# A Fourier and expert-layer kernel: dummy rows and half of a table sent later, float64 decoding in five VectorE operations instead of seven

## The chip, the cores and the metric

The kernel runs on one core of a Trainium2 chip. The metric is the time of one execution on the device in microseconds (us), as the median of several runs.

## What is computed

Three stages follow one another. `x` is 8 batches of 3072 tokens of 256 numbers.

```python
X = np.fft.fft(np.fft.fft(x, axis=1), axis=2).real      # attention stage
do_compute = x @ w_skip > 0                             # mixture of experts, 8 experts of 256 -> 1024 -> 256
e_idx = np.argmax(xc @ w_gate, axis=1)                  # for the rows xc that compute
y[mask] = gate_w[mask, None] * (np.maximum(xc[mask] @ w1[e], 0.0) @ w2[e])
out[do_compute] = xc + y
h = x @ w_in                                            # last layer, 256 -> 2048 -> 256
g = (a0 + a1*h + a2*h**2 + a3*h**3) / (1 + |b0|*|h| + |b1|*h**2 + 1e-6)
return g @ w_out
```

`w_in` and `w_out` come as float64; the kernel reads them as pairs of 32-bit words.

## The kernel before

There are two phases. The first computes the Fourier transform of all 24576 tokens, decides the expert of each and scatters the rows into a table in HBM (`xs`), sorted by expert. The second reads the rows back and runs experts and last layer; it fills the time from about 408 us on. The change is in the first phase, but for one loop count at the start of the second.

Products are made in float16 pairs: each float32 value is split into a high part (ScalarE, `AF.Copy`) and a low part (VectorE or GpSimd, a subtraction), and three matmuls are added up.

**The first phase.** `load_x(c)` loads block `c` (a 96x1024 tile; 8 blocks make a batch) from SP's queue into one of four buffers, so block `c+4` can be issued when the split of block `c` is done. `split_hi` (L190; L188 first where GpSimd makes the low part) and `split_lo` (L200 on VectorE, L198 on GpSimd for three blocks of each batch from block 12 on) split it. `s1(c)` is the first part of the transform, 24 matmuls; `s1_hi` (L231) and `s1_lo` (L238 on VectorE for blocks 0 to 6, afterwards two matmuls L241 and L242 on ScalarE) take the result out. A lead-in loop does this for the eight blocks of batch 0. It also issues the four pieces of the twiddle table `twt`.

Then come 98 steps `n` (12 per batch and two more). Step `n` stands for batch `n // 12` and its step `n % 12`, called step 0 to 11 of the batch here. It runs `s2` of two groups of tokens (12 matmuls L256, taken out by L260 on ScalarE and L261 on VectorE), `s3` of the step two before (12 matmuls, L305 to L307; L311 on ScalarE; L312 to L314 on VectorE), and in two of three steps a block of the next batch: `load_x`, `s1`, `split_hi`, and `split_lo` a step later. `s3` needs piece `k` of the twiddle table from the batch's step `3k + 2` on. Four PSUM buffers (`u`) are shared by all these.

**Work on the side** is written as Python generators; a step takes one or more pieces (calls) of each. Engines take their instructions in the order in which they are written, so the place of a piece among the others counts.

- `route_steps(bb)`: from step 1 of the next batch on, one piece per step: maximum, one-hot (L330 to L332), ranks by 25 matmuls (L336, L338), row numbers (L354), then two indirect scatters from GpSimd's queue per step (L357), 24 in all. Scatters need the dummy rows (`dum`), written from SP's queue to `xs` first. Row buffers are reused ten row tiles later, so `s3` writes (L312) wait for scatters.
- `decode_steps()`: `w_in` and `w_out` in eight items of 1024 columns: load from SP's queue (L374, L376), VectorE operations L391 to L398 that make a float32 of two words, ScalarE's high part L402, VectorE's low part L404, and the write to `wd` from ScalarE's queue (L406). Six calls make an item. Then eight items of the first two experts' weights, two calls each (load L415 or L417, high part L426, low part L428, write L430). 64 calls are spread evenly over steps 5 to 87. Loads and the `ws` tile that is written have two buffers each.
- `coefficients()`: tiny operations (L570) from step 12 on.

## Time and profile before

| | us |
|---|---|
| median of three runs | 3132.73 |
| lowest and highest run | 3129.66, 3134.80 |
| the profiled execution, its own time | 3128.56 |
| its span, first to last instruction | 3126.5 |
| TensorE busy in the span | 2981.5 (95%) |
| VectorE busy | 2701.1 (86%) |
| ScalarE busy | 2523.4 (81%) |
| GpSimd busy | 1392.4 (45%) |

The busy time of an engine is that of its instructions, overlaps counted once. All times in the rows are from the start of the span. PE is TensorE, DVE VectorE, ACT ScalarE, POOL GpSimd and SP the engine whose queue issues most transfers; ACTq and SPq are the queues' own issues. A share of the whole span is a mean over phases with different limits, so the rows below are from stretches of the first phase.

### The profile page before, as it was taken

To read this page: it belongs to the slowest core of one execution; us is meant where nothing else is said; L and a number is where in the kernel's file an instruction comes from. 1 tells how busy PE (TensorE), PEld (TensorE's weight loads), DVE (VectorE), ACT (ScalarE), POOL (GpSimd) and SP (SyncE) were. 2 spreads that over 40 slices of the span, in tenths; PEclk is the share of its full clock that TensorE was granted. 3 is DMA by queue.
4 is the path that set the end of the run, shared out by engine and by line. 5 is a ranking of instruction groups with operands and counts; after the bars stand their busy time and mean duration, and the time that the engine had idled before them with its cause. 6 is when DMAs were issued, how large, how long until landed. Compare 5 with 4: busy or idle time off the path is not lost.

```text
span 3126.5 us, 57696 instructions
## 1 busy us (share of the span) xinstructions
PE 2981.5 (95%) x23586; PEld 2198.1 (70%) x23586; DVE 2701.1 (86%) x2929; ACT 2523.4 (81%) x2694; POOL 1392.4 (45%) x796
## 2 busy tenths in 40 slices
PE   6899879998999999999999999999999999999996
PEld 5777647776767777777777777777777777777764
DVE  5999788999888898989888788898889888888886
ACT  5777667887888888878888788888888888888884
POOL 0467665443343444434444444444434444344444
PEclk9999989999999999999999999999999999999998
DMA  8556743121111221112112100020011000200000
GB/s 210 170 175 181 239 136 102 31 82 58 35 55 31 75 65 34 55 58 72 41 36 73 38 28 22 13 80 11 28 48 43 23 11 28 75 18 15 11 11 14
DMA packets 75617, 198.09 MB, mean 63 GB/s; under 512 B 12243, under 2 KB 36180, under 8 KB 72404
## 3 DMA queue, kind: packets, MB, share of 16 engines
q1 hardware_dynamic: 54612, 135.42, 14.5%
q0 software_dynamic: 18432, 50.55, 4.6%
q10 hardware_dynamic: 2304, 8.39, 0.7%
q8 instruction: 186, 3.05, 0.4%
q14 instruction: 83, 0.68, 0.1%
HBM read 190.69 MB, written 77.05 MB: 86 GB/s over the span
## 4 chain that ended last, share of the span: by engine, by line
PE 73%; DVE 12%; ACT 6%; issue 4%; DMA 3%; POOL 1%; SPq 0%; ACTq 0%; POOLq 0%; DVEq 0%
PE u L886 34%; PE accz L896 26%; PE acc L896 9%; DVE gh L995 3%; DVE T L977 2%; PE u L256 2%; DMA out<-ob,ids 1%; PE ut L876 1%; DVE V L1000 1%; ACT Y L976 1%; ACT T L975 1%; DMA xt<-in_x 1%; POOL xs L357 1%; DVE gl L1007 1%; ACT V L981 1%
## 5 line engine op out<-in xcount | busy, mean ns | idle before, releaser
L1001 POOL TENSOR_TENSOR V<-T,V 128x1024 f32<-128x1024 f32 x384 | 911.9, 2375 | 1395.6 <-DVE V L1000 1345.9
L896 PE MATMUL accz<-wo,gh 128*128 128x256 f16 x6144 | 1031.5, 273 | 2.8 <-ACT ob L1023 2.8
L886 PE MATMUL u<-th,wi 128*128 128x512 f16 x3072 | 984.1, 382 | 37.3 <-DVE T L977 31.2
L896 PE MATMUL accz<-wo,gl 128*128 128x256 f16 x3072 | 839.3, 273 | 14.5 <-DVE gl L1007 13.7
L886 PEld LDWEIGHTS <-wi 128*128 128x128 f16 x4608 | 453.2, 98 | 509.9 <-issue 54.5
L977 DVE SCALAR_TENSOR_TENSOR T<-T,co,u 128x1024 f32<-128x1024 f32 x384 | 490.2, 1277 | 303.5 <-ACT Y L976 299.0
L896 PEld LDWEIGHTS <-gh 128*128 128x128 f16 x6144 | 602.7, 98 | 155.5 <-issue 5.1
L975 ACT ACTIVATE T<-u,co 128x1024 f32<-128x1024 f32 x384 | 462.9, 1206 | 280.4 <-PE u L886 266.0
L995 DVE SCALAR_TENSOR_TENSOR gh<-T,co,Y 128x1024 f16<-128x1024 f32 x384 | 650.0, 1693 | 0.0
L886 PE MATMUL u<-tl,wi 128*128 128x512 f16 x1536 | 586.6, 382 | 0.1
L1007 DVE SCALAR_TENSOR_TENSOR gl<-V,co,Y 128x1024 f16<-128x1024 f32 x384 | 489.4, 1275 | 20.3 <-POOL V L1001 20.3
L1000 DVE SCALAR_TENSOR_TENSOR V<-V,co,gh 128x1024 f32<-128x1024 f32 x384 | 490.1, 1276 | 0.0
L985 ACT ACTIVATE Y<-V,co 128x1024 f32<-128x1024 f32 x384 | 443.1, 1154 | 0.0
L981 ACT ACTIVATE V<-Y,co 128x1024 f32<-128x1024 f32 x384 | 440.9, 1148 | 0.3 <-DVE gl L1007 0.3
L976 ACT ACTIVATE Y<-u,co 128x1024 f32<-128x1024 f32 x384 | 428.1, 1115 | 0.0
L989 ACT ACTIVATE Y<-Y 128x1024 f32<-128x1024 f32 x384 | 404.8, 1054 | 0.0
L896 PEld LDWEIGHTS <-gl 128*128 128x128 f16 x3072 | 301.3, 98 | 53.2 <-DVE gl L1007 16.4
L886 PE MATMUL u<-th,mw 128*128 128x256 f16 x1664 | 293.1, 275 | 10.6 <-DMA mw<-wd 5.6
L1024 POOL DMA_INDIRECT out<-ob,ids x192 | 225.7, 1175 | 125.4 <-ACT ob L1023 73.5
L896 PE MATMUL acc<-mw,hh 128*128 128x256 f16 x1664 | 278.1, 273 | 0.0
L886 PEld LDWEIGHTS <-mw 128*128 128x128 f16 x2496 | 246.0, 99 | 41.3 <-DMA mw<-wd 6.1
L930 ACT ACTIVATE hh<-u 128x1024 f16<-128x1024 f32 x104 | 106.5, 1024 | 158.3 <-PE u L886 158.3
(207 smaller groups left out, 3542.4 us busy)
## 6 DMA issues: line engine op xcount, KB each, us to landing
mw<-wd SPq DMA_DIRECT2D x50, 2048.0 KB
xt<-in_x SPq DMA_DIRECT2D x64, 384.0 KB
xm<-xs SPq DMA_DIRECT2D x52, 258.0 KB
wf<-in_moe_w SPq DMA_DIRECT2D x48, 256.0 KB
wd<-ws SPq DMA_DIRECT2D x48, 256.0 KB
xt<-xs SPq DMA_DIRECT2D x22, 516.0 KB
wd<-ws ACTq DMA_DIRECT2D x16, 512.0 KB
wr<-in_moe_w_in SPq DMA_DIRECT2D x4, 1024.0 KB
```

The costliest lines, as they stand in the source:

```text
L886: pe.matmul(u[:, s, :], lhsT=sta, rhs=mv[:, k, :], start=(n == 0), stop=(n == 5))
L896: pe.matmul(acc[:, r, :], lhsT=sta[:, c], rhs=mv, start=(first and r % 2 == 0 and s == 0 and n == 0), stop=(last and s == nf - 1 and n == ...
L975: act.activation(d["T"], d["u"], AF.Square, scale=A[0], bias=A[1])
L976: act.activation(d["Y"], d["u"], AF.Abs, scale=A[4])
L977: dve.scalar_tensor_tensor(out=d["T"], in0=d["T"], scalar=A[2], in1=d["u"], op0=ALU.add, op1=ALU.mult)
L981: act.activation(d["V"], d["Y"], AF.Square, bias=A[5])
L985: act.activation(d["Y"], d["V"], AF.Ln, bias=A[6])
L989: act.activation(d["Y"], d["Y"], AF.Exp, scale=-1.0)
L995: dve.scalar_tensor_tensor(out=h[:], in0=d["T"], scalar=A[a0], in1=d["Y"], op0=ALU.add, op1=ALU.mult)
L1000: dve.scalar_tensor_tensor(out=d["V"], in0=d["V"], scalar=A[c], in1=h[:], op0=ALU.add, op1=ALU.mult)
L1001: pool.tensor_tensor(out=d["V"], in0=d["T"], in1=d["V"], op=ALU.subtract)
L1007: dve.scalar_tensor_tensor(out=l[:], in0=d["V"], scalar=A[a0], in1=d["Y"], op0=ALU.add, op1=ALU.mult)
```

## The change

1. The five writes of dummy rows, issued ahead of the steps before, are issued in steps 5, 7, 9, 11 and 13. Of the four pieces of the twiddle table two are issued in the lead-in (after blocks 5 and 7) and two in steps 2 and 4. The cosine table `csb` is issued ahead of blocks 2 and 3, and the copies from it stand ahead of three other small VectorE operations. The first weight load of the decoding is issued ahead of the steps.
2. In the lead-in, the low parts of blocks 3 and 5 go by the way of L241 and L242 instead of L238.
3. Decoding: a ScalarE pass (`AF.Abs`) takes the place of the masking L397; the sign bit and the exponent's top bit are kept by other masks, and the exclusive-or L395 is gone. Five calls make an item, with the low part and the write in one. An item of the experts' weights takes one call: low part, write, a load two items on, and the high part of the next item.
4. The calls are made one per step in steps 2 to 11 of batch 0, and from then on twice in step 0, once in steps 1 and 6 and twice in step 9 of each batch.
5. The routing has an empty piece between the one-hot and the matmuls that read it, so what follows comes a step later. The second phase takes one more piece of the last batch's routing at its start.

```diff
@@ s1_lo
-                if c < 7:
+                if c < 7 and c not in (3, 5):
@@ route_steps, behind the one-hot
             yield
+            yield
             u = new_u()
@@ decode_steps
             nxt = load(0)
+            yield
             for n in range(8):
...
-                m = wp.tile([128, 1024], I32, tag="wm", name="wm")
+                m = wp.tile([128, 1024], F32, tag="wm", name="wm")
-                dve.tensor_scalar(out=fi, in0=hw, scalar1=3, scalar2=0x7FFFFFFF, op0=ALU.logical_shift_left, op1=ALU.bitwise_and)
-                dve.scalar_tensor_tensor(out=fi, in0=hw, scalar=-0x80000000, in1=fi, op0=ALU.bitwise_and, op1=ALU.bitwise_or)
+                act.activation(m[:], hw.bitcast(F32), AF.Abs)
+                dve.tensor_scalar(out=fi, in0=hw, scalar1=3, scalar2=0x3FFFFFFF, op0=ALU.logical_shift_left, op1=ALU.bitwise_and)
+                yield
+                dve.scalar_tensor_tensor(out=fi, in0=hw, scalar=-0x40000000, in1=fi, op0=ALU.bitwise_and, op1=ALU.bitwise_or)
                 yield
                 dve.scalar_tensor_tensor(out=fi, in0=lw, scalar=29, in1=fi, op0=ALU.logical_shift_right, op1=ALU.bitwise_or)
-                dve.tensor_scalar(out=fi, in0=fi, scalar1=0x40000000, scalar2=None, op0=ALU.bitwise_xor)
-                yield
-                dve.tensor_scalar(out=m[:], in0=hw, scalar1=0x7FFFFFFF, scalar2=None, op0=ALU.bitwise_and)
-                dve.scalar_tensor_tensor(out=f[:], in0=m[:], scalar=float(0x38100000), in1=f[:], op0=ALU.is_ge, op1=ALU.mult)
+                if n + 1 < 8:
+                    nxt = load(n + 1)
                 yield
+                dve.scalar_tensor_tensor(out=f[:], in0=m[:], scalar=TINY, in1=f[:], op0=ALU.is_ge, op1=ALU.mult)
                 act.activation(st[:, 0, :], f[:], AF.Copy, scale=sc)
                 yield
                 dve.scalar_tensor_tensor(out=st[:, 1, :], in0=f[:], scalar=sc, in1=st[:, 0, :], op0=ALU.mult, op1=ALU.subtract)
-                yield
                 act.dma_start(out=WD[E + n // 4, :, n % 4, :, :], in_=st[:])
                 yield
...
+            pend = hi()
+            yield
+            for n in range(4 * EARLY):
+                t, st = pend
                 dve.scalar_tensor_tensor(out=st[:, 1, :], in0=t, scalar=256.0, in1=st[:, 0, :], op0=ALU.mult, op1=ALU.subtract)
-                yield
                 act.dma_start(out=WD[n // 4, :, n % 4, :, :], in_=st[:])
+                if n + 2 < 4 * EARLY:
+                    loads.append(load_e(n + 2))
+                if loads:
+                    pend = hi()
+                yield
@@ lead-in
-            if c >= 4:
-                g = 6 * (c - 4)
-                sp.dma_start(out=twt[:, g:g + 6], in_=tw[:, g:g + 6])
+            if c in (5, 7):
+                load_tw(c // 7)
@@ steps
-            while decoded < min(n_dec, (n - 3) * n_dec // 84):
-                next(prep, None)
-                decoded += 1
+            for _ in range(1 if n < 12 else DECODE.get(gp, 0)):
+                if n >= 2:
+                    next(prep, None)
+            if n in (2, 4):
+                load_tw(2 + n // 4)
+            if n in (5, 7, 9, 11, 13):
+                dummies((n - 5) // 2)
```

`DECODE` is `{0: 2, 1: 1, 6: 1, 9: 2}`, and `TINY` is the float32 with the bits 0x38100000.

Three places show how this moves instructions. The first is SP's queue from block 4 of x to the first weight loads (`xt` is a block of x, `twt` the table, `dum` the dummy rows, `wr` a weight load). Before:

```order
L178 DMA xt<-in_x 96x1024
L585 DMA twt<-const_tw 128x3072
L589 DMA xs<-dum 512x1x258 x4
L591 DMA xs<-dum 768x1x258
L178 DMA xt<-in_x 96x1024 x4
L374 DMA wr<-in_moe_w_in 128x2048 x2
L178 DMA xt<-in_x 96x1024 x6
```

And with the change:

```order
L180 DMA xt<-in_x 96x1024 x6
L584 DMA twt<-const_tw 128x3072
L180 DMA xt<-in_x 96x1024 x2
L584 DMA twt<-const_tw 128x3072
L377 DMA wr<-in_moe_w_in 128x2048
L180 DMA xt<-in_x 96x1024 x2
L584 DMA twt<-const_tw 128x3072
L180 DMA xt<-in_x 96x1024 x2
L377 DMA wr<-in_moe_w_in 128x2048
L584 DMA twt<-const_tw 128x3072
L589 DMA xs<-dum 512x1x258
```

The `x4` block of x behind the five dummy writes is that of blocks 12 to 15. With the change, block 12 is the first behind the first weight load, and the first dummy write stands behind block 15.

The second place is VectorE in step 3 of batch 3, the one-hot of the routing (L330 to L332 before, L332 to L334 after). Before:

```order
L314 TENSOR_TENSOR rt<-ev,u 128x18
L330 TENSOR_TENSOR rt<-rt 128x24x8
L331 TENSOR_SCALAR rt<-rt 128x24
L332 TENSOR_TENSOR rt<-rt,smt 128x216
L397 TENSOR_SCALAR wm<-wr 128x1024
L398 SCALAR_TENSOR_TENSOR wf<-wm,wf 128x1024
L570 TENSOR_TENSOR co<-co,rt 128x1
L261 SCALAR_TENSOR_TENSOR o2l<-u,o2h 128x552
```

With the change, this step and the next:

```order
L332 TENSOR_TENSOR rt<-rt 128x24x8
L333 TENSOR_SCALAR rt<-rt 128x24
L334 TENSOR_TENSOR rt<-rt,smt 128x216
L580 TENSOR_TENSOR co<-co,rt 128x1
L263 SCALAR_TENSOR_TENSOR o2l<-u,o2h 128x552
L314 TENSOR_TENSOR mw_71<-ev,u 128x2x129
L315 TENSOR_TENSOR mw_71<-ev,u 128x2x127
L316 TENSOR_TENSOR rt<-ev,u 128x18
L580 TENSOR_SCALAR co<-co 128x1
L580 RECIPROCAL rt<-co 128x1
L263 SCALAR_TENSOR_TENSOR o2l<-u,o2h 128x552
```

The two decoding operations behind the one-hot are gone from the step, and the step after it holds no routing.

The third is ScalarE at the end of a step with an expert's weights in batch 6. Before:

```order
L190 ACTIVATE xh<-xt 96x1024
L430 DMA wd<-ws 128x2048
L426 ACTIVATE ws<-wr 128x1024
L231 ACTIVATE o1h<-u 128x192x4
L260 ACTIVATE o2h<-u 128x552
```

With the change, step 9 of that batch, which has two calls:

```order
L313 ACTIVATE ev<-u 128x276
L434 DMA wd<-ws 128x2048
L426 ACTIVATE ws<-wr 128x1024
L434 DMA wd<-ws 128x2048
L426 ACTIVATE ws<-wr 128x1024
L233 ACTIVATE o1h<-u 128x192x4
```

The second write and the second high part now stand between the first ones and the next step's evictions, and each write waits for the low part that VectorE makes in the same call.

## Rows read from the trace of the kernel before

**Rows 1.** Busy us (instructions) per stretch; then granted clock, DMA share, GB/s.

```profile
0.00:30.00 30.00, 16.84 (x218) 15.91 (x219) 19.04 (x33) 17.30 (x19) 1.06 (x8) 1.00 0.87 226
30.00:63.20 33.20, 21.57 (x225) 16.75 (x224) 9.64 (x18) 16.20 (x23) 2.12 (x1) 0.79 1.05 255
63.20:83.70 20.50, 20.08 (x249) 16.57 (x248) 20.07 (x36) 16.88 (x26) 0.00 (x0) 1.00 0.30 79
83.70:109.20 25.50, 22.23 (x274) 18.03 (x273) 21.46 (x64) 19.23 (x30) 7.10 (x3) 1.00 0.43 136
109.20:128.80 19.60, 19.56 (x249) 16.53 (x249) 18.71 (x42) 16.51 (x25) 11.64 (x10) 1.00 0.64 204
128.80:156.40 27.60, 22.18 (x274) 18.05 (x273) 24.92 (x67) 20.51 (x31) 20.01 (x16) 1.00 0.64 192
...
176.00:204.30 28.30, 23.49 (x274) 19.07 (x273) 23.30 (x63) 20.22 (x32) 21.70 (x18) 0.94 0.58 190
...
224.30:249.10 24.80, 22.10 (x274) 18.02 (x273) 23.66 (x64) 20.13 (x33) 19.07 (x15) 1.00 0.69 197
...
269.10:297.80 28.70, 22.23 (x275) 18.10 (x274) 27.20 (x65) 20.59 (x31) 21.62 (x17) 1.00 0.51 153
...
317.70:345.70 28.00, 23.65 (x274) 18.95 (x273) 19.98 (x59) 20.84 (x32) 22.68 (x19) 0.94 0.74 225
345.70:366.50 20.80, 19.86 (x249) 16.58 (x249) 17.15 (x37) 15.86 (x24) 11.46 (x12) 1.00 0.49 166
...
390.40:408.00 17.60, 15.23 (x175) 13.23 (x172) 13.17 (x40) 8.09 (x17) 9.75 (x10) 1.00 0.45 159
...
500.00:3126.50 2626.50, 2566.36 (x18989) 1866.64 (x18986) 2293.91 (x1994) 2179.25 (x2210) 1118.69 (x568) 0.99 0.13 42
```

The five busy times are those of TensorE's matmuls, its weight loads, VectorE, ScalarE and GpSimd.

**Rows 2.** Timeline of ScalarE, 0 to 110 us: start, us; [idle before <- releaser].

```profile
54.21 1.06 ACT L188 ACTIVATE xt<-xt 96x1024 f32<-96x1024 f32 x1 [11.02 <-DMA xt<-in_x]
```

**Rows 3.** Timeline of SP's queue, 18 to 60 us: start, us.

```profile
26.07 9.49 SPq L589 DMA_DIRECT2D xs<-dum  x4
35.61 2.19 SPq L591 DMA_DIRECT2D xs<-dum  x1
37.90 5.14 SPq L178 DMA_DIRECT2D xt<-in_x  x4
```

**Rows 4.** Groups of VectorE, 30 to 410 us: busy us, mean ns | idle before.

```profile
L397 DVE TENSOR_SCALAR wm<-wr 128x1024 int32<-128x1024 int32 x8 | 9.8, 1231 | 0.0
L392 DVE SCALAR_TENSOR_TENSOR wf<-wr,wf 128x1024 int32<-128x1024 int32 x8 | 9.8, 1226 | 0.3
L398 DVE SCALAR_TENSOR_TENSOR wf<-wm,wf 128x1024 f32<-128x1024 int32 x8 | 9.8, 1226 | 0.3
...
L391 DVE TENSOR_SCALAR wf<-wr 128x1024 int32<-128x1024 int32 x8 | 5.7, 718 | 0.0
L395 DVE TENSOR_SCALAR wf<-wf 128x1024 int32<-128x1024 int32 x8 | 5.6, 703 | 0.3
```

**Rows 5.** Groups of ScalarE's decoding, 30 to 410 us.

```profile
L426 ACT ACTIVATE ws<-wr 128x1024 f16<-128x1024 f32 x8 | 8.4, 1050 | 7.9 <-DMA wd<-ws 6.1 <-DVE ws L428 1.8
L402 ACT ACTIVATE ws<-wf 128x1024 f16<-128x1024 f32 x8 | 8.4, 1049 | 3.8 <-DVE wf L398 3.8
```

**Rows 6.** Group of TensorE's routing matmuls, 30 to 410 us.

```profile
L336 PE MATMUL u<-rt,utt 128*128 128x216 f16 (+7 forms) x168 | 11.9, 230 | 11.6 <-DVE rt L332 7.6 <-DVE o2l L261 4.0
```

**Rows 7.** Timelines of VectorE and of GpSimd, 194 to 198 us.

```profile
194.77 3.10 DVE L397 TENSOR_SCALAR wm<-wr 128x1024 int32<-128x1024 int32 x1
...
195.16 2.15 POOL L198 TENSOR_TENSOR xl<-xt,xh 96x1024 f16<-96x1024 f32 x1
```

**Rows 8.** Timeline of ScalarE, 368 to 384 us.

```profile
369.81 0.34 ACTq L430 DMA_DIRECT2D wd<-ws  x1
...
381.52 1.06 ACT L426 ACTIVATE ws<-wr 128x1024 f16<-128x1024 f32 x1 [6.07 <-DMA wd<-ws]
```

**Rows 9.** Timeline of VectorE in step 3 of batch 6, 312 to 396 us.

```profile
335.63 2.75 DVE L331 TENSOR_SCALAR rt<-rt 128x24 f16<-128x24 f32 x1
```

More of the change, by code (lines that the diff above doesn't have):

```diff
@@ L38 @@
 CB = 276
+TINY = float(np.int32(0x38100000).view(np.float32))
+DECODE = {0: 2, 1: 1, 6: 1, 9: 2}
 def split16(v):
@@ L380, in decode_steps @@
             nxt = load(0)
-            pend = None
+            yield
             for n in range(8):
                 t = nxt
-                if n + 1 < 8:
-                    nxt = load(n + 1)
                 v = t[:].rearrange("p (n two) -> p n two", two=2)
@@ L450, in program @@
             split_x(c)
-        dve.tensor_copy(out=carry[:], in_=smt[:, 0:9])
-        dve.tensor_copy(out=wgh[:, :, 0, :], in_=wgf[:])
-        dve.tensor_tensor(out=wgh[:, :, 1, :], in0=wgf[:], in1=wgh[:, :, 0, :], op=ALU.subtract)
         for h in range(2):
@@ L457, in program @@
                 dve.tensor_copy(out=f2t[:, h, mv, 147:276], in_=csb[:, h, mv, 1, 0:129])
+        dve.tensor_copy(out=carry[:], in_=smt[:, 0:9])
+        dve.tensor_copy(out=wgh[:, :, 0, :], in_=wgf[:])
+        dve.tensor_tensor(out=wgh[:, :, 1, :], in0=wgf[:], in1=wgh[:, :, 0, :], op=ALU.subtract)
         def gate_columns():
@@ L571, in coefficients, with load_tw, dummies @@
                 yield
+        def load_tw(k):
+            sp.dma_start(out=twt[:, 6 * k:6 * k + 6], in_=tw[:, 6 * k:6 * k + 6])
+        def dummies(r):
+            if r < R0:
+                sp.dma_start(out=XS[SKIP0 + r * TILE:SKIP0 + (r + 1) * TILE, :].rearrange("(p r) c -> p r c", p=128),
+                             in_=dum[:, None, :].to_broadcast([128, 4, ROW]))
+            else:
+                sp.dma_start(out=XS[0:R1 * HALF, :].rearrange("(p r) c -> p r c", p=128), in_=dum[:, None, :].to_broadcast([128, R1 * HALF // 128, ROW]))
         for c in range(8):
@@ L582, in program @@
                 gate_columns()
-            if c >= 4:
-                g = 6 * (c - 4)
-                sp.dma_start(out=twt[:, g:g + 6], in_=tw[:, g:g + 6])
+            if c in (5, 7):
+                load_tw(c // 7)
         s1_hi()
         s1_lo()
-        for r in range(R0):
-            sp.dma_start(out=XS[SKIP0 + r * TILE:SKIP0 + (r + 1) * TILE, :].rearrange("(p r) c -> p r c", p=128),
-                         in_=dum[:, None, :].to_broadcast([128, 4, ROW]))
-        sp.dma_start(out=XS[0:R1 * HALF, :].rearrange("(p r) c -> p r c", p=128), in_=dum[:, None, :].to_broadcast([128, R1 * HALF // 128, ROW]))
         late = []
@@ L594, in program @@
         coeff = coefficients()
-        n_dec = 8 * 6 + 4 * EARLY * 2
-        decoded = 0
+        next(prep)
         c1 = 8
@@ L1158, in program @@
                 if i == 0:
-                    next(last)
-                    next(last)
+                    for _ in range(3):
+                        next(last)
             if 0 <= i - 1 < total:
```

18 lines of the change are left out of this document (9 added, 9 removed).

## The prediction

> **What bounds the kernel now.** I read the table of stretches first, cut at the start of the Fourier steps, six steps to a row [rows 1]. From 500 us to the end TensorE works in 2566.4 of 2626.5 us, and the change touches nothing there. Whatever it does happens in the first 408 us or so, and since the last stage is TensorE's own pace, time saved ahead of it should come out at the end.
>
> In those 408 us three things stand out. The six steps from 30.0 to 63.2 us take 33.2 us, and TensorE works in 21.6 of them; the next six take 20.5. From there on the second halves of the batches, which carry no routing besides its last two pieces, take 19.6 us in batch 1 and 20.8 in batch 6, with TensorE busy nearly throughout: this is the floor of six steps. The first halves, which carry the routing, take 25.5, 27.6, 28.3, 24.8, 28.7 and 28.0 us, on the mean 27.2, with TensorE busy in 22.2 to 23.7 of each.
>
> The timeline of ScalarE says why the early stretch is long: it waits 11.0 us for a block of x and goes on at 54.2 [rows 2]. The timeline of SP says where the block was: SP issues the five writes of dummy rows from 26.07 on, needs 9.49 us for the first four and 2.19 for the fifth, and reaches the next blocks of x at 37.90 only [rows 3]. In the same stretch DMA is busy throughout (share 1.05, 255 GB/s) [rows 1].
>
> The long first halves are VectorE's and the coupling's. VectorE is busy in 21.5 to 27.2 us of those of batches 1 to 5, and decoding is part of it: seven operations per item, with the means of [rows 4] (L394 as L392, L404 as L398) 7.6 us together. TensorE's routing matmuls take 11.9 us in seven batches, 1.7 per batch, and waited 11.6 us in all [rows 6]. That wait falls in first halves alone.
>
> **The change part by part.**
>
> *Dummies and tables.* Up to the block that was late, the trace moved 30 us at 226 GB/s and 24 us at 255, some 12.9 MB [rows 1]. By the shapes of the tiles the change takes 2.9 MB of dummies and half of 3.1 MB of table from ahead of that block and puts one 1.05 MB load of weights there: 3.4 MB less, which at 255 GB/s is 13 us. The block, which landed at 54.2, then lands near 41 us by that count, and earlier if SP issues it earlier, since SP stood 11.7 us in the dummies [rows 3]. ScalarE asked for it at 43.2 us (54.2 less 11.0). So the wait should go whole. The six steps then cost what the next six do, 20.5 us with decoding in them, a gain of 12.7; the low clock granted in that stretch (0.79 on the mean, so a part of it at 1.2 GHz) goes with the idle time. Bounds: 11.0, the wait alone, and 13.6, down to the floor of 19.6. I take 12.5. What is late next: the dummies now go out singly in steps 5 to 13 between blocks of x that are loaded two to three steps ahead, and must land before the first scatter in step 20, seven steps after the last of them, some 23 us at 19.6 us for six. I cost this at nothing; without that cover POOL's scatters would start late by the time of one write, 0.8 MB at 255 GB/s or 3 us. The third and fourth table pieces are issued in steps 2 and 4 and needed in steps 8 and 11.
>
> *The prelude.* One table piece (3 us at 255 GB/s) no longer stands ahead of a late block, the copies of the cosine table run before VectorE waits for small constants, and two subtractions go from VectorE to TensorE and ScalarE. TensorE is busy in 16.8 of 30.0 us there [rows 1]. I take 1 us; bounds -1 and 2.
>
> *Decoding.* Gone are two VectorE operations per item, L395 and L397, 0.70 and 1.23 us; the others stay [rows 4]. ScalarE gets one more pass of the size of L402, 1.05 us [rows 5]. Over eight items VectorE loses 15.5 us of work and ScalarE gains 8.4. VectorE is on the path only where routing lies beside decoding, so the place counts more than the sum. Before, 64 calls are spread over 84 steps, 4.6 to a half batch: at 7.6/6 us, 5.8 us of VectorE in a first half. After, three calls (two in step 0, one in step 1) of 5.6/5 us: 3.4 us. VectorE's mean in batches 1 to 5 of 24.1 us becomes 21.7, below TensorE's 22.2. Nothing of decoding remains in steps 2 to 5, where the one-hot and the ranks are made, and the added yield gives VectorE a whole step between the one-hot and the matmuls that read it. The halves ran 2.9 us over VectorE's busy time. Between 22.2, where all lies beside TensorE, and 26, where ScalarE's new passes in steps 0 and 1 eat the most of it, I take 24.0, nearer the first since the second halves show six steps running at TensorE's pace with VectorE 95% busy. Gain 3.0 us each (27.0 less 24.0), five batches: 15; bounds 5 and 24.
>
> One row shows what else the moved operations met: L397 in step 3 of batch 3 took 3.10 us while GpSimd's subtraction beside it took 2.15 [rows 7]; L395, of the same kind and size, has a mean of 0.70 [rows 4]. So 2.4 us of it was a standstill. In step 3 of batch 6, where no decoding stands, a small routing operation, L331, took 2.75 us [rows 9]. I keep the 15, since most batches have no such row, and the case in which the standstill passes to the next operation is a rival below. The Trainium skill (SBUF — State Buffer, Who interferes with whom) has VectorE and GpSimd share one port pair that one of them holds for a whole instruction while the other stands still. Both rows agree with it.
>
> *Weights of the experts.* These now take one call each instead of two: VectorE's low part, the write on ScalarE's queue, the next load, and ScalarE's next high part. Where two calls stand in one step (batch 6, steps 0 and 9; batch 7, step 0), ScalarE waits in its own order for VectorE (1.2 us) and then for a buffer whose write was issued just before. Behind it stand the evictions that TensorE needs. The trace has such a wait once: write at 369.81, its buffer free at 381.52, ScalarE idle for 6.07 of that [rows 8]. This was beside the 4 MB of weights that the next stage loads; so I take 3 us of standstill at the first two places, half of it hidden by ScalarE's spare time (it is busy in 20.8 of 28.0 us [rows 1]), against the 3 us that batch 6 wins as the others do: 0, with another -1 for chains of VectorE, ScalarE and VectorE in batches 4 and 5. Bounds -7 and 2.
>
> *The tail.* The wait of 6.07 us in batch 7 becomes one of the same kind two steps earlier: nothing. The added yield puts the last scatters one step later, and the last Fourier steps wait for those rows, so the stage ends one short step later: 17.6 us for eight steps [rows 1], 2.2 each. I take -2; bounds -6 and 3.
>
> **Sum:** 12.5 + 1 + 15 - 1 - 2 = 25.5 us. The profiled execution took 3128.56 us (span 3126.5), so 3103.1. The median of the three runs, 3132.73, stands 4.2 above it, so **3107**.
>
> **The rivals.** A difference within 0.2% (6.3 us) can't be told from no change here.
>
> - *Only the stall goes.* The first halves stay at 27 us, because ScalarE in steps 0 and 1 (two passes per block for GpSimd, now a decode pass or a wait for VectorE more) sets them and not VectorE. For it: the first half of batch 6 had VectorE busy in 20.0 us only and still took 28.0 [rows 1]. Against it: ScalarE had 7 us free there. The sum is 12.5 + 1 - 1 - 2 = 10.5: 3122.
> - *The block of x is late again.* The weight load ahead of it and the table pieces hold it as the dummies did. For it: DMA is the limit up to 63 us (share 1.05), and the count above leaves only 2 us. Against it: SP is free 11 us earlier. With half the wait left the sum is 25.5 - 5.5 = 20: 3113; with all of it, 13: 3120.
> - *The standstill at the port is passed on.* GpSimd still subtracts beside steps 1 to 4 of each batch, and what stood still in [rows 7] and [rows 9] is followed by other VectorE operations. At 2.4 us in each of five batches the sum is 25.5 - 12 = 13.5: 3119. The rule named above would have it so; the rows show it in some batches only.
> - *Slower.* The double calls of the expert weights. If each of the three places holds ScalarE as long as that one write took, 11.7 us, and TensorE with it, this costs 35 less the 6 lost before: 29, against the 25.5 of the sum, so 3136. It decides from some 10.5 us of TensorE's time at each place. Against it: L426's eight have 6.1 us of waits for a buffer in total, all from that one place [rows 5].
>
> **How the numbers follow.** Forecast (sum 18 to 36) 0.60; only the stall 0.18; port passed on 0.07; block late again 0.07; slower 0.04, half of it by over 6.3 us; part gains of several lost, down to within 6.3 us, 0.04. The range reaches from 3096, where the halves get near 22.5 us, to 3122, which takes in all rivals but the slower one; what is below or above holds some 0.2. The forecast's own range is 3097 to 3115. Faster 0.92, same 0.06, slower 0.02.
>
> **What would show it.** Right: no wait of ScalarE for x near 43 us and the first six steps near 20.5 us; first halves of batches 1 to 5 near 24 us with TensorE busy in over 90%; second halves at 20; the first stage ending near 383 us instead of 408; the rest unchanged at 2718 us. Wrong: waits of ScalarE for L428's or L404's counterpart ahead of a write in steps 0, 1 and 9, or for a buffer in batches 6 and 7; rows of x waited for after 35 us; or a last stage that starts early and then waits, for the fills of the row table or for expert weights, and gives the time back.

## The result and the profile after

| | us |
|---|---|
| changed kernel, median (lowest to highest of 4 runs) | 3167.24 (3162.78 to 3168.07) |
| kernel before, beside it (4 runs) | 3133.08 (3129.66 to 3134.80) |
| ratio, 95% interval | 1.0107 (1.0090 to 1.0125) |
| profiled execution, its span | 3168.07, 3165.9 |

The change is 34 us slower; 3107 was forecast. The profile after, by stretches that begin at the same Fourier steps as those of [rows 1] (busy us of TensorE's matmuls, its weight loads, VectorE, ScalarE and GpSimd; then granted clock, DMA share, GB/s):

```profile
31.70:53.00 21.30, 20.70 (x225) 16.52 (x224) 11.85 (x21) 16.91 (x24) 2.48 (x1) 0.87 0.77 246
53.00:81.40 28.40, 22.72 (x249) 18.20 (x248) 19.54 (x35) 18.41 (x28) 0.00 (x0) 0.88 0.71 203
81.40:107.10 25.70, 23.16 (x275) 18.68 (x274) 19.00 (x50) 20.63 (x31) 7.21 (x3) 0.93 0.55 155
107.10:134.20 27.10, 23.06 (x250) 18.63 (x248) 18.57 (x55) 16.86 (x25) 10.53 (x10) 0.87 0.40 123
...
187.00:217.10 30.10, 24.46 (x274) 19.75 (x273) 20.12 (x48) 21.13 (x33) 20.95 (x17) 0.89 0.57 178
217.10:236.90 19.80, 19.72 (x253) 16.59 (x250) 17.65 (x53) 15.93 (x24) 12.46 (x12) 1.00 0.61 191
...
369.50:403.90 34.40, 24.08 (x253) 19.29 (x250) 17.81 (x49) 16.24 (x24) 22.43 (x22) 0.80 0.53 177
...
540.00:3165.90 2625.90, 2566.62 (x19004) 1867.50 (x19001) 2295.92 (x1997) 2178.36 (x2210) 1116.47 (x569) 0.99 0.13 42
```

The last row says that the second phase is what it was (2626.5 us before for the same stretch, 2566.4 of TensorE). The first six steps take 21.3 us in place of 33.2: the stall is gone. But the next six take 28.4 where they took 20.5, and the same goes on. The Fourier steps begin 1.7 us later than before; then, against before: first six steps -11.9, next six +7.9, first halves of batches 1 to 5 together +8.2 (25.7, 31.4, 30.1, 28.9, 27.0), their second halves +16.2 (27.1, 21.4, 19.8, 22.2, 24.8, where 19.6 to 20.0 was the rule), batch 6 +15.3, the first half of batch 7 +1.8. That is 39.2 of the span's 39.4 us. More work is not the reason: in most of these stretches VectorE, the suspected one, is busy less than before, and over the span it is busy 15.0 us less (2686.1). ScalarE has 7.9 us more (2531.3), its added pass. TensorE is busy 18.7 us more with the same matmuls; why these take longer stands in the last section.

So it is waits. The groups of the changed kernel, 30 to 420 us, that answer to [rows 5] and [rows 6], with three more (busy us, mean ns | idle before, and what ended it). The window ends in the midst of the last batch's routing, so L339 and L263 lack their last 24 and 10 instructions; up to 460 us L339's idle time is 0.0 still, and L263's is 103.0, of which 102.8 for `o2h`.

```profile
L243 PE MATMUL u<-o1h,nid 128*128 128x384 f16 x114 | 50.8, 551 | 54.0 <-ACT o1h L233 53.5
L339 PE MATMUL u<-rt,utt 128*128 128x216 f16 (+7 forms) x144 | 9.5, 219 | 0.0
...
L190 ACT ACTIVATE xt<-xt 96x1024 f32<-96x1024 f32 x19 | 19.9, 1046 | 0.0
L404 ACT ACTIVATE ws<-wf 128x1024 f16<-128x1024 f32 x8 | 8.4, 1056 | 14.7 <-DVE wf L401 14.7
L426 ACT ACTIVATE ws<-wr 128x1024 f16<-128x1024 f32 x8 | 8.4, 1052 | 20.6 <-DVE ws L433 8.3 <-DMA wr<-in_moe_w 4.7 <-DMA wd<-ws 4.7
...
L263 DVE SCALAR_TENSOR_TENSOR o2l<-u,o2h 128x552 f16<-128x552 f32 x86 | 62.7, 729 | 100.1 <-ACT o2h L262 99.8
```

The first and the last of these in the kernel before, 30 to 410 us:

```profile
L241 PE MATMUL u<-o1h,nid 128*128 128x384 f16 x113 | 46.8, 515 | 21.7 <-ACT o1h L231 21.2
L261 DVE SCALAR_TENSOR_TENSOR o2l<-u,o2h 128x552 f16<-128x552 f32 x96 | 69.8, 727 | 61.2 <-ACT o2h L260 60.8
```

Two waits are gone as forecast: ScalarE's for x (L190, 11.0 before) and TensorE's routing matmuls' (L339, 11.6 before). In their place ScalarE waits in its decoding: 14.7 us at the high part (3.8 before) and 20.6 at the experts' (7.9). Behind that come the evictions: TensorE waits 53.5 us for ScalarE's `o1h`, where it waited 21.2 before, and VectorE 99.8 us for `o2h` (60.8 before). One such place, the end of step 0 of batch 3, in the timeline of all engines (L233, L243 and L263 are those of step 1):

```profile
191.62 1.06 ACT L192 ACTIVATE xh<-xt 96x1024 f16<-96x1024 f32 x1
191.82 1.22 DVE L397 SCALAR_TENSOR_TENSOR wf<-wr,wf 128x1024 int32<-128x1024 int32 x1
192.82 2.19 POOL L200 TENSOR_TENSOR xl<-xt,xh 96x1024 f16<-96x1024 f32 x1 [0.30 <-issue]
193.07 3.03 DVE L401 SCALAR_TENSOR_TENSOR wf<-wm,wf 128x1024 f32<-128x1024 f32 x1
196.13 1.06 ACT L404 ACTIVATE ws<-wf 128x1024 f16<-128x1024 f32 x1 [3.44 <-DVE wf L401]
197.42 0.79 ACT L233 ACTIVATE o1h<-u 128x768 f16<-128x768 f32 x1
198.26 1.44 PE L243 MATMUL u<-o1h,nid 128*128 128x384 f16 x2 [4.93 <-ACT o1h L233]
198.76 0.73 DVE L263 SCALAR_TENSOR_TENSOR o2l<-u,o2h 128x552 f16<-128x552 f32 x1 [2.67 <-ACT o2h L262]
```

ScalarE had nothing to do with L401 but to read what it makes. Its high part L404 stands in the same call, so ScalarE, which takes its instructions in order, stood still for 3.44 us until VectorE got there. Behind L404 stands L233, for which TensorE waits 4.93 us; and behind that the eviction for which VectorE itself then waits 2.67 us. L401 took 3.03 us here, where L397, of the same size, took 1.22: it began 0.25 us behind GpSimd's subtraction, which ended at 195.01, and 1.1 us after that end it was done. The Trainium skill (SBUF — State Buffer, Who interferes with whom) has the later of the two wait at their shared port pair for the whole instruction of the first; this place agrees. In [rows 7] VectorE's operation has the earlier start on record (194.77 against 195.16) and stood still all the same, so there the order of the starts does not say who waits.

ScalarE's timeline, with the issues on its queue (ACTq), at step 9 of batch 6, where two calls for the experts stand:

```profile
388.84 0.36 ACTq L434 DMA_DIRECT2D wd<-ws  x1
389.30 1.06 ACT L426 ACTIVATE ws<-wr 128x1024 f16<-128x1024 f32 x1 [2.82 <-DVE ws L433]
391.64 0.39 ACTq L434 DMA_DIRECT2D wd<-ws  x1
395.04 1.06 ACT L426 ACTIVATE ws<-wr 128x1024 f16<-128x1024 f32 x1 [4.69 <-DMA wd<-ws]
396.01 0.79 ACT L233 ACTIVATE o1h<-u 128x768 f16<-128x768 f32 x1
```

ScalarE stands idle 2.82 us over the first write, which waits for its low part, and 4.69 us ahead of the second high part, which waits for a buffer whose write was issued 6.2 us before it starts (388.84). TensorE waits 7.70 us for the L233 at the end.

### The profile page after: what moved, and what is told of

The parts are those of the page before. It is cut to its first block, busy times and chain, and to the rows that moved or that the text cites. A ratio compares the mean times of both kernels' runs of the same rounds, so it can differ in the third digit from the quotient of the medians.

```text
span 3165.9 us, 57687 instructions
## 1 busy us (share of the span) xinstructions
PE 3000.2 (95%) x23590; PEld 2209.1 (70%) x23590; DVE 2686.1 (85%) x2911; ACT 2531.3 (80%) x2704; POOL 1381.5 (44%) x796
## 4 chain that ended last, share of the span: by engine, by line
PE 73%; DVE 12%; ACT 7%; issue 4%; DMA 2%; POOL 1%; ACTq 0%; SPq 0%; DVEq 0%; POOLq 0%
PE u L905 33%; PE accz L915 25%; PE acc L915 9%; DVE gh L1014 2%; PE u L258 2%; DVE T L996 2%; PE ut L895 1%; DMA out<-ob,ids 1%; DVE V L1019 1%; ACT Y L995 1%; ACT T L994 1%; PE u L243 1%; DVE gl L1026 1%; ACT o1h L233 1%; ACT V L1000 1%
## 5 line engine op out<-in xcount | busy, mean ns | idle before, releaser
L915 PE MATMUL accz<-wo,gl 128*128 128x256 f16 x3072 | 839.0, 273 | 15.5 <-DVE gl L1026 14.7
```

What stands on the lines that cost most here:

```text
L915: pe.matmul(acc[:, r, :], lhsT=sta[:, c], rhs=mv, start=(first and r % 2 == 0 and s == 0 and n == 0), stop=(last and s == nf - 1 and n == ...
```

## The experiments

Theory A: a ScalarE instruction (a high part, or the issue of a write) in the call of the VectorE operation that it waits for holds ScalarE, and so the evictions behind it. Theory B: it is the double calls and their crowding in steps 0, 1 and 9. Theory C: ScalarE's added pass. Theory D, which came up later, is on the empty routing piece. The kernels ran in five groups, each beside the kernel before; its medians were 3129.6, 3238.7, 3129.5, 3129.2 and 3128.8 us. What is compared across groups is the ratio; a ratio step of 0.001 is 3.1 us. All of them compute the whole.

**First group.** e1 takes points 1 and 2 of the change alone (but for the first weight load, which stays where it was); e4 adds the empty routing piece:

```diff
# e1: as the change, without
-            yield                       (empty routing piece)
-  five-operation decode_steps, DECODE  (those of before, 64 calls evenly)
# e4: e1 and
+            yield                       (empty routing piece)
```

> The kernel before with the first two points of the change alone: dummy rows and half of the table later, cosine table earlier, blocks 3 and 5 by the other way. Decoding, its pace and the routing are those of before. Both theories (the loss sits in the decoding's calls; the loss sits in the dummy writes and table pieces that now lie among the steps) differ here. If the loss is in the decoding, the stall of 11 to 13 us goes and nothing else: 3119 to 3123 us. If the later dummies and table pieces collide with blocks of x or scatters, part of the 12.7 us is given back: 3127 us or more.

Measured: 3115.32 us, ratio 0.9955 (0.9938 to 0.9971): 14 us faster, a little more than I expected. The early part is a clear gain, and the later dummies cost nothing that shows.

> As the first kernel of this call, with the empty routing piece and its one more piece at the start of the second phase. In the changed kernel's trace steps 4 and 5 of the batches lost some 2.5 us less each than before, so I expect 12 to 15 us below the first kernel of this call, 3105 to 3110 us; if the matmuls that waited there only shift the wait to the next step, it is as fast as that kernel within 3 us.

Measured: 3132.26 us, 1.0011 (1.0001 to 1.0020). Neither: the empty piece costs 17 us.

```diff
# e2: the changed kernel, with
-            for _ in range(1 if n < 12 else DECODE.get(gp, 0)):
+            want = max(0, n - 1) if n < 12 else 10 + (n - 11) * 39 // 74
+            while decoded < want:
# e3: the changed kernel, with ScalarE's instructions of w_in and w_out a call later
+                if n:
+                    lo(*pend)                      (low part, with the next item's first call)
                 act.activation(m[:], hw.bitcast(F32), AF.Abs)
...
                 yield
+                if n:
+                    write(pend[0], pend[1])        (write, a call behind the low part)
...
                 dve.scalar_tensor_tensor(out=f[:], in0=m[:], scalar=TINY, in1=f[:], op0=ALU.is_ge, op1=ALU.mult)
+                yield                              (high part, a call behind the comparison)
                 act.activation(st[:, 0, :], f[:], AF.Copy, scale=sc)
```

> The changed kernel with its calls spread evenly: one per step in steps 2 to 11, then 39 over the next 74 steps, never two in a step. Each call is the same as in the changed kernel. Theory A (a ScalarE instruction that waits for a VectorE operation of its own call holds ScalarE's evictions, wherever the call stands): the standstills go with the calls to other steps, and the time stays above 3145 us, less what batch 6 loses where two writes follow one another in step 9 (up to 9 us). Theory B (it is the two calls in one step, and the three in steps 0 and 1): most of the loss is gone, 3110 us or less.

Measured: 3146.94 us, 1.0054 (1.0037 to 1.0070). Spreading alone takes back half of what the changed kernel lies over before, 17 us, where B asked for 3110 us or less. Its decoding still waits (ScalarE 18.2 us at the high part), so B alone does not hold.

> The changed kernel, with its steps and its double calls, but in the eight items of w_in and w_out no ScalarE instruction stands in the call of the VectorE operation that it waits for: the high part comes a call after the last comparison, the low part in the next item's first call, the write a call after that. The experts' items stay. Theory A: batches 0 to 5 lose what they gained in excess over TensorE's own pace, by steps some 35 us, and batches 6 and 7 keep theirs: 3120 to 3135 us. Theory B (two calls in a step): no change, 3160 us or more. Theory C (ScalarE's added pass, the absolute value, is what fills ScalarE): no change either.

Measured: 3142.09 us, 1.0046 (1.0029 to 1.0063), by the ratios 19 us less than the changed kernel, though 3120 to 3135 us was expected. ScalarE's wait at the high part falls from 14.7 to 2.8 us; that at the experts' stays at 20.0, and TensorE's for `o1h` falls from 53.5 to 36.1:

```profile
L415 ACT ACTIVATE ws<-wf 128x1024 f16<-128x1024 f32 x8 | 8.4, 1046 | 2.8 <-DVE wf L411 2.8
L243 PE MATMUL u<-o1h,nid 128*128 128x384 f16 x114 | 47.0, 514 | 36.7 <-ACT o1h L233 36.1
```

**Second group, on one other chip.** The four kernels of the next group ran on a chip on which all took some 100 us more, the kernel before beside them included. In their traces several engines stand idle at once in steps 5 to 7, 10 and 11, with no releaser that the trace names. What makes this stays open. All four were run again on another chip, so only their expectations and ratios stand here.

```diff
# e5: e3, 58 calls spread evenly (step 5 on), each expert item in two calls (low part | write, load, next high part)
# e6: e5 without the empty routing piece
# e8: the changed kernel without the empty routing piece
# e9: the changed kernel, each expert item in two calls, one call per step from batch 6 on
```

> Early part, empty routing piece and the five-operation decoding, with every ScalarE instruction a call behind the VectorE operation that it waits for, the experts' items in two calls each as in the kernel before, and the 58 calls spread evenly over steps 5 to 87. Against e4_early_and_yield (3132 us) only the decoding's operations differ. If VectorE's saved time (some 15 us over the stage) counts once no wait stands in ScalarE's order, 3117 to 3124 us; if five operations with ScalarE's added pass bring nothing, 3130 us or more.

> As the kernel above it in this call, without the empty routing piece. Against e1_early_only (3115 us) only the decoding's operations differ. If the five operations are a gain by themselves, 3100 to 3110 us; if nothing, 3113 to 3118 us. The difference to the kernel above is the empty piece: in e4 against e1 it cost 17 us, so 17 us less if that holds whatever the decoding, less than 5 if it was the meeting of one comparison with GpSimd's subtraction in batch 2.

> The changed kernel without the empty routing piece and its one more piece in the second phase. If the piece costs what e4 lost against e1, 3150 us. If the steps' own times in the changed kernel hold (steps 4 to 6 took 2.4 us less per batch than before, and only the end of the stage came later), 3170 to 3180 us.

> The changed kernel with the experts' items in two calls each (low part; then write, next load and high part) and one call per step from batch 6 on. By theory A batches 6 and 7, which stand 25 and 13 us over TensorE's own pace, come to about 10 each as in the kernel before: 3147 to 3154 us. If these losses come from elsewhere (the expert weights that the next phase loads, the write's own time), no change: 3162 us or more.

Measured on that chip: e5 0.9964 (0.9950 to 0.9978), e6 0.9963 (0.9946 to 0.9980), e8 1.0112 (1.0084 to 1.0139), e9 1.0082 (1.0053 to 1.0110). e5 does the changed kernel's work in another arrangement of calls and lies below the kernel before, which says already that the arrangement is worth the whole loss; the finer differences can't be read here.

**Third group.** The strongest test of A adds the suspected cost to a fast kernel. e10 is e1, and only ScalarE's two instructions per item of `w_in` and `w_out` stand a call earlier; the order of TensorE, VectorE, GpSimd and SP is that of e1, row for row:

```diff
                 dve.scalar_tensor_tensor(out=f[:], in0=m[:], scalar=float(0x38100000), in1=f[:], op0=ALU.is_ge, op1=ALU.mult)
-                yield
                 act.activation(st[:, 0, :], f[:], AF.Copy, scale=sc)
                 yield
+                yield
                 dve.scalar_tensor_tensor(out=st[:, 1, :], in0=f[:], scalar=sc, in1=st[:, 0, :], op0=ALU.mult, op1=ALU.subtract)
-                yield
                 act.dma_start(out=WD[E + n // 4, :, n % 4, :, :], in_=st[:])
                 yield
+                yield
```

> e1_early_only with seven operations, the same pace and the same order on TensorE, VectorE, GpSimd and SP: only ScalarE's two instructions of each of the eight items of w_in and w_out (the high part, and the issue of the write) stand one call earlier, in the call of the VectorE operation that they wait for. Theory A: 16 instructions, each of which holds ScalarE by up to one VectorE operation and what stands ahead of it (1.2 to 5 us), so 15 to 40 us over e1, a ratio to the kernel before of 1.000 to 1.008. If waits of this kind are hidden, as e1 within 0.1%.

Measured: 3170.94 us, 1.0135 (1.0118 to 1.0151). That is 0.0180 over e1, or 56 us for 16 instructions moved by one call: A, and more than I expected of it. The same groups in e1's trace:

```profile
L404 ACT ACTIVATE ws<-wf 128x1024 f16<-128x1024 f32 x8 | 8.4, 1049 | 3.0 <-DVE wf L400 2.9
L243 PE MATMUL u<-o1h,nid 128*128 128x384 f16 x114 | 46.6, 510 | 12.8 <-ACT o1h L233 12.3
L263 DVE SCALAR_TENSOR_TENSOR o2l<-u,o2h 128x552 f16<-128x552 f32 x96 | 69.8, 727 | 49.6 <-ACT o2h L262 49.2
```

and in e10's:

```profile
L403 ACT ACTIVATE ws<-wf 128x1024 f16<-128x1024 f32 x8 | 8.4, 1056 | 32.8 <-DVE wf L400 32.8
L243 PE MATMUL u<-o1h,nid 128*128 128x384 f16 x114 | 51.0, 554 | 49.0 <-ACT o1h L233 48.5
L263 DVE SCALAR_TENSOR_TENSOR o2l<-u,o2h 128x552 f16<-128x552 f32 x87 | 63.5, 730 | 94.1 <-ACT o2h L262 93.9
```

And the longest of these waits of ScalarE in e10's timeline, where the one-hot of batch 3's step 3 stands:

```profile
206.64 1.06 ACT L192 ACTIVATE xh<-xt 96x1024 f16<-96x1024 f32 x1
207.30 0.72 DVE L263 SCALAR_TENSOR_TENSOR o2l<-u,o2h 128x552 f16<-128x552 f32 x1
208.80 2.42 DVE L332 TENSOR_TENSOR rt<-rt 128x192 f16<-128x192 f32 x1
...
212.70 1.22 DVE L400 SCALAR_TENSOR_TENSOR wf<-wm,wf 128x1024 f32<-128x1024 int32 x1
213.96 1.06 ACT L403 ACTIVATE ws<-wf 128x1024 f16<-128x1024 f32 x1 [6.26 <-DVE wf L400]
214.92 0.79 ACT L233 ACTIVATE o1h<-u 128x768 f16<-128x768 f32 x1
215.76 1.44 PE L243 MATMUL u<-o1h,nid 128*128 128x384 f16 x2 [6.80 <-ACT o1h L233]
216.26 0.73 DVE L263 SCALAR_TENSOR_TENSOR o2l<-u,o2h 128x552 f16<-128x552 f32 x1 [2.27 <-ACT o2h L262]
```

ScalarE runs ahead of VectorE. An instruction that reads VectorE's newest result makes it wait not for one operation but for all that VectorE still has before it (here from 207.70, where L192 ends, to 213.92, where L400 does), the evictions behind it come late, and then VectorE has nothing to do either.

```diff
# e11: the changed kernel, with
-                act.activation(m[:], hw.bitcast(F32), AF.Abs)
+                dve.tensor_scalar(out=m[:].bitcast(I32), in0=hw, scalar1=0x7FFFFFFF, scalar2=None, op0=ALU.bitwise_and)
# e12, e13: the kernels e5 and e6
```

> The changed kernel with the absolute value made by VectorE (a masking of the kernel before's kind) in place of ScalarE's pass, so six VectorE operations. Theory C (ScalarE's added passes of 1.05 us fill ScalarE): some 8 us or more below the changed kernel, a ratio of 1.008 or less. Theory A: ScalarE's waits for VectorE stay and VectorE has 0.7 to 1.2 us more in each, so as the changed kernel or up to 10 us slower, 1.010 to 1.015.

Measured: 3160.49 us, 1.0095 (1.0078 to 1.0112). This lies between what C and A asked for. The intervals overlap with the changed kernel's; ScalarE's pass, set against the work that VectorE gets in its place, is worth some 4 us by the medians, so C does not make the loss of 34.

> The same kernel as e5_five_ops_even_yield, for a second chip, since all four kernels of that call, the kernel before among them, took 100 us more there than elsewhere. As expected there: 3117 to 3124 us at 3130 for the kernel before if the saved VectorE time counts, 0.996 to 0.998.

> The same kernel as e6_five_ops_even_no_yield, for a second chip. As expected there: 0.990 to 0.994 if five operations are a gain over e1 (0.9955), 0.995 to 0.996 if not; and the empty routing piece costs what the kernel above it lies higher.

Measured: e12 3129.54 us, 1.0000 (0.9991 to 1.0010); e13 3111.75 us, 0.9946 (0.9929 to 0.9963). Five operations against seven with the same pace: e12 3.4 us under e4, e13 2.8 under e1, which is within the intervals; e12 misses the 0.996 to 0.998 that I expected. The empty piece costs 17 us again. Where it comes from stands in VectorE's group that writes the rows of the third pass, here e12's:

```profile
L314 DVE TENSOR_TENSOR mw<-ev,u 128x258 f32<-128x258 f32 x56 | 23.1, 413 | 8.3 <-DMA xs<-mw,rt 7.0 <-ACT ev L313 1.3
L314 DVE TENSOR_TENSOR third<-ev,u 128x258 f32<-128x258 f32 x40 | 16.5, 414 | 5.3 <-DMA xs<-third,rt 4.6 <-ACT o1h L233 0.6
```

and e13's:

```profile
L314 DVE TENSOR_TENSOR mw<-ev,u 128x258 f32<-128x258 f32 x56 | 23.1, 412 | 1.3 <-DMA xs<-mw,rt 0.9 <-ACT ev L313 0.4
L314 DVE TENSOR_TENSOR third<-ev,u 128x258 f32<-128x258 f32 x40 | 16.5, 412 | 1.3 <-DMA xs<-third,rt 1.3
```

VectorE waits 11.6 us for scatters that still read the row buffers, against 2.2.

**Fourth group.** e14 keeps the empty piece and makes the two pieces behind the matmuls one, so the second phase begins with two pieces of routing as without it; e15 takes only the write of e10; e16 and e17 are e8 and e9.

```diff
# e14: e12, with
             dve.tensor_scalar(out=carry[:, 0:1], ...)
-            yield
             dve.tensor_tensor(out=rk, in0=rk, in1=oh, op=ALU.mult)
# e15: of e10's edit only the second half
```

> e12 with the empty routing piece kept, and the two pieces behind the matmuls (ranks; row numbers) made one, so that the scatters stand in the same steps as without the empty piece. Theory D (the empty piece costs 17 us because the scatters come a step later and the third pass writes its rows into buffers that are not yet scattered: VectorE waits 11.6 us for them in e12, 2.2 in e13): the cost goes and the gain of steps 4 to 6 stays, 0.990 to 0.995 of the kernel before. Rival (the matmuls in step 5 meet more work there): as e12, 0.999 to 1.001.

Measured: 3116.12 us, 0.9953 (0.9937 to 0.9970), 15 us under e12; the waits of VectorE for scatters are 3.3 us. So the cost was the scatters' place (D). But the gain of the empty piece does not show: e13, without it, is as fast or a little faster, though TensorE's routing matmuls wait 6.8 us there and 0.3 in e14.

> e1_early_only with only the write's issue of the eight items a call earlier, in the call of the low part that it waits for; the high part where it was. In e10 both stood a call earlier and cost 55 us. By the waits in its trace (32.8 us of ScalarE at the high part against 3.0) I expect the smaller share from the write, 10 to 20 us: 0.999 to 1.002. If the issue of a write does not hold ScalarE, 0.995 to 0.996.

Measured: 3133.14 us, 1.0012 (1.0002 to 1.0022): 18 us over e1 for eight writes, 2.2 each, and so by difference some 38 us of e10's 56 for eight high parts.

> The same kernel as e8_change_without_yield, for another chip. If the empty piece costs 17 us here too, 1.005; if its gain in steps 4 to 6 and its cost even out in the changed kernel, where VectorE waits only 2.2 us for rows, 1.009 to 1.013 as on the chip before.

Measured: 3164.99 us, 1.0114 (1.0097 to 1.0130). In the changed kernel the empty piece costs and brings nothing that shows (1.0107 with it).

> The same kernel as e9_change_expert_calls_split, for another chip. Theory A: 13 to 20 us below the changed kernel, 1.004 to 1.006; as on the chip before, 1.008.

Measured: 3149.10 us, 1.0060 (1.0043 to 1.0077), 15 us under the changed kernel. Batch 6 of e17 by halves, where the changed kernel took 29.7 and 34.4 us:

```profile
338.00:362.60 24.60, 21.87 (x274) 18.08 (x273) 16.44 (x47) 21.90 (x32) 15.43 (x12) 1.00 0.68 223
362.60:383.60 21.00, 19.71 (x253) 16.58 (x249) 17.91 (x49) 16.23 (x24) 14.15 (x13) 1.00 0.63 188
```

e17 changes two things, the double calls and the write in the low part's call. e2's batch 6 has single calls too, but low part, write and next high part in one:

```profile
328.90:360.00 31.10, 24.91 (x274) 19.86 (x273) 18.37 (x48) 22.71 (x33) 17.85 (x15) 0.89 0.66 204
360.00:388.40 28.40, 23.01 (x254) 18.43 (x250) 17.34 (x49) 15.64 (x24) 15.55 (x16) 0.88 0.46 142
```

That is 59.5 us, against 64.1 in the changed kernel and 45.6 in e17: by these traces most of this batch's loss is that write and high part stand in the low part's call, and the smaller part the double calls.

**Fifth group.** The last question was what the placement itself is worth, with neither waits in ScalarE's order nor double calls:

```diff
# e18: e13, 58 calls evenly over steps 2 to 11 and then over all steps but 3 and 4 of a batch
# e19: e13, with
-            while decoded < min(58, (n - 3) * 58 // 84):
+            if 2 <= n < 12 or n >= 12 and gp in (0, 5, 6, 7, 8, 9, 10, 11):
                 next(prep, None)
```

> e13 (no empty piece, five operations, ScalarE a call later, 0.9946), with no decoding call in steps 3 and 4 of batches 1 to 6, where the one-hot and the matmuls that read it stand. If VectorE's decoding there is what still delays these matmuls (steps 4 take 2.6 to 3.7 us over TensorE's other work in e13, of which the routing matmuls are 1.7), 1 to 1.5 us per batch: 0.991 to 0.993. If not, 0.994 to 0.996.

Measured: 3112.30 us, 0.9944 (0.9924 to 0.9963): no gain over e13.

> As e18, with the calls of batches 1 to 6 in steps 0 and 5 to 11 alone, so one in each of these steps: the place that the change is named after, without its waits of ScalarE and without double calls. If keeping decoding out of the routing's steps is a gain, as I predicted (3 us per batch), 0.989 to 0.992. If the second halves, where VectorE was busy in 18.7 of 19.6 us before, now lose what the first gain, 0.994 to 0.997.

Measured: 3103.84 us, 0.9916 (0.9899 to 0.9932): 25 us under the kernel before, the fastest of all; 9 us under e13, whose interval it just meets, and 8 us under e18, which ran beside it and whose lowest run (3107.85) is above its highest (3105.01). Its stretches, the first half of batch 2, which is the slowest, and batch 3 by halves:

```profile
115.40:145.00 29.60, 24.71 (x274) 19.48 (x273) 22.75 (x63) 18.86 (x29) 19.43 (x16) 0.88 0.52 162
...
165.50:189.40 23.90, 21.92 (x275) 18.05 (x274) 19.04 (x60) 20.32 (x33) 19.65 (x15) 1.00 0.67 205
189.40:210.10 20.70, 19.87 (x249) 16.56 (x249) 20.23 (x44) 17.36 (x26) 16.39 (x14) 1.00 0.69 199
```

## Why the prediction was wrong

- **The stall (12.5 us): right.** There is no wait of ScalarE for x and no price of the later dummies that shows. The first six steps take 21.3 us in the changed kernel and 19.8 in e1, where 20.5 was forecast; e1, with the prelude, gains 14.
- **The prelude (1 us): not borne out.** The steps begin at 31.7 us instead of 30.0, in e1 at 31.3; but in e17, whose lead-in is the changed kernel's, at 30.4, so a microsecond can't be read here.
- **First halves (15 us): the step that failed.** I took a decoding call to be so many microseconds of VectorE, and took it from the stretches in which VectorE is the bound. The calls' ScalarE instructions I priced at their own 1.05 us. What they cost is where they stand. In the kernel before, each stood a call, so some 1.3 steps, behind the operation that it reads, and [rows 5] showed what that leaves: 3.8 us for L402. The change put them into the same call, and the 3.8 became 14.7. The diff showed it (a `yield` gone between the low part and its write, the comparison and the high part in one piece). My text prices such chains in batches 4 and 5 alone, at 1 us. The first rival has a wait of ScalarE for VectorE in steps 0 and 1, but nothing above what the halves took before, and the signs of being wrong name one ahead of a write; none names the high part. e3 says 19 us for those of `w_in` and `w_out`; e10 shows that the same fault alone can cost 56. And I looked at the half batches that calls were taken from: those that got them, the second halves and steps 6 to 11 of batch 0, I put at no loss, and they lost 16.2 and 7.9 us. In e3 they take 20.7 us on the mean (23.1 in the changed kernel) and 20.2 (28.4), so most of that loss is the same waits. The first halves themselves take 27.5 us in e3, not the 24.0 of the forecast (27.0 before): VectorE's waits for scatters, 8.5 us in all, are left there, and what else holds them was not tried. (A reading that is off by little: TensorE's busy time in the first halves starts at 22.1 us in [rows 1], not at 22.2.)
- **Experts' weights (-1 us): right place, wrong size.** I counted 3 us of standstill at each of two places and half of it hidden; batch 6 lost 15.3 us, and e17, which takes the writes out of the low parts' calls and the double calls apart, gives back 15 over all. That was my slower rival's mechanism, which I gave 0.04, with 29 us. It came true at half its price, beside the larger one that was not among the rivals.
- **The empty piece (-2 us): wrong place, and in a kernel without the other waits some eight times too small.** I looked for its cost at the end of the stage, and for its gain in the first halves. But the scatters, one step later in every batch, meet row buffers that the third pass wants again: 17 us in e4 and e12, gone in e14. In the changed kernel it costs nothing that shows (e16); that this is because its third pass is late itself was not tried. The wait of the routing matmuls did go, as forecast, but e14 and e13 are level, so that this wait cost little.
- **The other rivals.** The block of x was not late again. The standstill at the port went on but grew no dearer: before, ten operations of VectorE beside GpSimd's subtractions took over 0.6 us more than the median of their kind (same line and shape), 19.2 us in all; in the changed kernel eight, 13.9 us. What is new is that ScalarE waits behind some of them.
- **The placement, seen alone, is a gain.** In e19 the first halves of batches 1 to 5 take 25.6 us on the mean (24.6, 29.6, 23.9, 24.5, 25.2; 27.1 in e1; forecast 24.0) and the second 20.7 (19.8 in e1). So in these batches the first halves win 7.8 us over e1 and the second lose 4.3, where I had forecast 15 and no loss; the rest of the 12 us between e1 and e19 falls in batch 0, batch 6 and the start of batch 7. And e19's place is one call in each of eight steps, not the change's own six calls in four steps.

Added up in ratios: the changed kernel 1.0107, less 0.0061 (e3) and 0.0047 (e17), gives 0.9999; e12, which has both cures and an even pace, has 1.0000. Each ratio in this sum has an interval of 0.0017 to either side, so that it agrees to 0.0001 is luck, and e17 takes double calls apart as well. This leaves little for the double calls by themselves (theory B), but it does not show that they cost nothing. e2 gained 17 us by spreading the same calls: its first halves of batches 1 to 5 take 26.5 us on the mean (28.6 in the changed kernel), its second 23.6 (23.1), batch 6 4.6 us less and the first half of batch 7 20.8 (25.7). That it takes the calls apart, or out of steps in which ScalarE has most to do: which of these, was not tried by itself. Without the empty piece it is 0.9946, with the placement 0.9916.

## What to carry to other kernels

Where engines run in order and ahead of one another, an instruction costs what stands behind it while it waits, not its own time: for each instruction that a change moves, ask how far its producer runs behind, and what is queued after it. Here an instruction that reads another engine's result belonged a step behind the one that makes it (e10, e3), and the issue of a DMA from a computing engine's queue counted as such an instruction (e15). A change of many parts should be tried part by part, since here a gain of 14 us and losses of 19, 15 and (once the others are cured) 17 us lay in one diff, and the placement that it was made for is worth some 9 us only in another form (e19).

## What the runs showed of the hardware

- TensorE's waits cost twice here, once as idle time and once as clock. The stretches around the wait of 4.93 us in step 1 of batch 3 (193.3 to 198.3 us), of the changed kernel:

```profile
188.00:193.30 5.30, 5.21 (x70) 4.66 (x71) 4.12 (x8) 3.06 (x5) 4.08 (x5) 1.00 0.93 286
193.30:198.20 4.90, 0.03 (x1) 0.00 (x0) 2.79 (x1) 2.04 (x5) 4.44 (x3) 0.93 0.82 269
198.20:204.00 5.80, 5.74 (x38) 4.02 (x38) 3.39 (x8) 4.58 (x8) 1.38 (x2) 0.50 0.26 103
```

Behind the idle time the granted clock is 0.50, the lower of the two levels (1.2 and 2.4 GHz), for 5.8 us in which TensorE is busy in 5.74; ahead of it, it was 1.00. The two matmuls L243 right behind the wait took 1.44 us; two such at 52.42 us, behind no wait, took 0.81. In the stretch with the longest waits (369.5 to 403.9 us) the mean granted clock was 0.80, so a part of it ran at the lower level, and the matmuls took 24.1 us of busy time, where before they took 19.9 [rows 1]. Over the span TensorE's busy time rose by 18.7 us (3000.2 against 2981.5), nearly half of the span's 39.4; in e10 by 24.7 over e1 (3001.7 against 2977.0).
- An issue of a write from ScalarE's queue that waits for its data held ScalarE as a computing instruction does: moved up to its low part, it cost 2.2 us for each of eight (e15), and in that trace ScalarE's queue waits up to 4.27 us at one of them.
- One group of runs, on one chip, took 3238.7 us for the kernel before, where it took 3129 to 3133 in all other groups. No second group ran on that chip, so whether it is the chip stays open.
